# K and V of an attention backward pass, loaded two heads to a transfer

## The chip, the cores and the metric

The kernel runs on one core of a Trainium2 chip. The metric is the device time in microseconds (us) of one execution of the program. The core has five engines that run side by side, each with its own queue of instructions: PE (matrix multiply; PEld is its weight load), DVE (vector work), ACT (scalar engine, used here for copies out of PSUM, one exponential and one scaled copy), POOL (a general engine, used here for a few small products and for issuing stores) and SP (which only issues transfers here). Transfers between the chip's memory (HBM) and the on-chip memory (SBUF, 128 partitions) are carried by 16 DMA engines, which all queues share.

## The reference

Forward and backward of softmax attention in which 32 query heads share 4 key/value heads, for 32 batches:

```python
B, Hq, Hkv, Sq, Sk, D = 32, 32, 4, 4, 2048, 128      # all bf16

def forward(q, k, v):
    k = jnp.repeat(k, Hq // Hkv, axis=1)
    v = jnp.repeat(v, Hq // Hkv, axis=1)
    scores = jnp.einsum("bhqd,bhkd->bhqk", q, k) * D ** -0.5
    p = softmax(scores, axis=-1)
    return jnp.einsum("bhqk,bhkd->bhqd", p, v)

out, vjp = jax.vjp(forward, q, k, v)
return out, *vjp(grad_out)                            # out, dq, dk, dv
```

q, out, grad_out and dq are 1 MB each. k, v, dk and dv are 67.1 MB each: K and V are read once and dK and dV are written once, and these four make up nearly all the traffic.

## The kernel before, in words

One batch is one unit of work. Its 32 query heads of 4 rows give 128 rows, which fill the 128 partitions; 32 rows belong to each of the 4 key/value heads. A head of K (2048 keys of 128 numbers) lies in SBUF as 16 keys to a partition: a partition holds 4 KB of the head, one unbroken piece in HBM, and the head is 512 KB. A batch's K tile has four heads side by side, 16 KB to a partition, 2 MB in all; V's tile has the same shape, and so have the output tiles of dK and dV.

For one batch b the steps are these, named as in the program's table. `LK`, `LV`: issue the loads of K and V. `QDT`: transpose q and grad_out on PE. `KT0` to `KT7` and `VT0` to `VT7`: transpose eight 128x128 blocks of K or V on PE into a bank of PSUM (line 181), then copy them to SBUF on DVE (line 183). An even number takes heads 0 and 1, an odd one heads 2 and 3: `turned` transposes four blocks of the first head of the pair and then four of the second. `Sa`, `Sb`: scores (line 198) and their maxima. `EXa`, `EXb`: the exponential on ACT. `NRM`: row sums, and scaled copies of q and grad_out on POOL. `ETa`, `ETb`: the exponentials transposed. `O`: the output (line 264, reads all of V's tile) and its row-wise product with grad_out. `dPa`, `dPb`: the product of grad_out with V, and dS on DVE (line 350). `dV0` to `dV7`: PE products (line 307), copied out of PSUM by ACT (line 311) into the dV tile. `dSTa`, `dSTb`: dS transposed. `dQ`: line 264 again, reads all of K's tile. `dK0` to `dK7`: as dV.

The order is written out by hand as three lists of step names, `HEAD`, `STEADY` and `TAIL`, and no planner changes it; every engine takes its own share of the steps in that order. `STEADY` is one iteration: steps marked `-` belong to the batch before, `+` to the next, `+2` to the one after that. Its core, as far as the change touches it:

```python
STEADY = """
dSTa- VT4 EXa VT0 QDT+ dSTb- KT4+ dK1- dK6- KT6+ KT2+ KT0+ NRM dK0- dQ- dK3- ... ETb ETa VT7 KT3+ VT6 VT1
dV7 dK4- O dV5 dPb dV1 KT5+ KT1+ dV3 dV6 dPa KT7+ dV2 LK+2 LV+2 VT2+ dV4 Sa+ dV0 Sb+ dK7 VT5+ VT3+ EXb+
"""
```

So the loads of batch b+2 stand at the end of iteration b, and the first transposes of its K (KT4) near the start of iteration b+1. SP has only loads in its queue, so it runs ahead of the other engines and is held by waits alone. There are two kinds. One is for a free buffer: the K tile has three buffers, so K of b+2 waits until `dQ` of b-1 has read its K; the V tile has two, so V of b+2 waits until `O` of b has read its V (and the transposes of V are done). The other is for a semaphore: the framework gives SP's transfers eight semaphores in turn, and a transfer is issued only when the one issued eight before it, which raises the same semaphore, has landed. A batch has eight transfers, so head h of K waits for head h of the batch before, and so with V.

Stores go out on POOL's queue (line 338: dK of a batch in one transfer of 2 MB with four 4 KB pieces to a partition, 512 KB apart in HBM; dV likewise, in some batches cut into parts). dK and dV tiles share four buffers. The first ACT copy into a tile needs the store of the tile four before it to have landed. Each group of four batches has its q and grad_out loaded at once, from SP for the first group and from POOL for the others.

Of the kernel before, what the change touches and what calls it, by code (L numbers as in the profile page):

```python
# [81 lines left out]
def kernel(ctx: ExitStack, tc: tile.TileContext, q, k, v, grad_out, out_0, out_1, out_2, out_3):  # L82
    nc = tc.nc
    B, Hq, Sq, D = q.shape
    NH, Sk = k.shape[1], k.shape[2]
# [41 lines left out]
    k_v = k.rearrange("b h (p c) d -> b h p (c d)", c=C)  # L127
    v_v = v.rearrange("b h (p c) d -> b h p (c d)", c=C)
# [8 lines left out]
    def GROUP(g, queue):  # L137

        groups[g] = []
        for name, src in (("q_sb", q_f), ("do_sb", go_f)):  # L140
            x = qd_pool.tile([P, W, D], BF16, name=name)
            queue.dma_start(out=x[:], in_=src[g * W:g * W + W].rearrange("w p d -> p w d"))
            groups[g].append(x)

    def LK(b):
        S = st[b] = {}
        if b == 0:
            GROUP(0, nc.sync)
        S["q"], S["do"] = (x[:, b % W, :] for x in groups[b // W])
        if b % W == W - 1 and b + 1 < B:  # L150
            GROUP(b // W + 1, nc.gpsimd)
        S["k"] = k_pool.tile([P, NH, C, D], BF16, name="k_sb")
        for h in range(NH):
            nc.sync.dma_start(out=S["k"][:, h].rearrange("p c d -> p (c d)"), in_=k_v[b, h])

    def LV(b):
        S = st[b]
        S["v"] = v_pool.tile([P, NH, C, D], BF16, name="v_sb")
        for h in range(NH):
            nc.sync.dma_start(out=S["v"][:, h].rearrange("p c d -> p (c d)"), in_=v_v[b, h])  # L160

    def bank16():

# [182 lines left out]
    def dP(b, i):  # L346
# [6 lines left out]
        banks.give(t)  # L353

    table = {"LK": LK, "LV": LV, "QDT": QDT, "O": O, "dQ": dQ, "NRM": NRM}
    for i, c in enumerate("ab"):
        for n, f in (("S", S_), ("EX", EX), ("dP", dP), ("ET", ET), ("dST", dST)):
# [8 lines left out]
    for w in STEADY.split():  # L366
        ahead = 0
        for mark, n in (("+3", 3), ("+2", 2), ("+", 1), ("-2", -2), ("-", -1)):
            if w.endswith(mark):
                w, ahead = w[:-len(mark)], n  # L370
# [3 lines left out]
    with tc.manual_schedule():  # L374

        for w in HEAD.split():
            w, b = w.split("@")
# [5 lines left out]
        for w in TAIL.split():  # L383
            w, b = w.split("@")
# [31 lines left out]
```

## Time and profile before

| what | value |
|---|---|
| median of three runs | 690.12 us (684.78 to 690.79) |
| the profiled execution, its own time | 688.33 us |
| span of its trace, first to last instruction | 686.5 us |
| granted TensorE clock, mean | 0.99 |
| PE / DVE / ACT busy | 621.9 / 584.8 / 569.1 us (91 / 85 / 83%) |
| HBM read and written | 136.31 MB and 136.31 MB, 397 GB/s over the span |
| loads of K and V | 128 and 128 transfers of 512 KB from SP's queue |

The profile is one execution. Busy times are sums over the whole span, and the stages of this kernel have different limits: a start that fills the pipeline, a long stretch of like iterations of some 20 us each, and an end in which nothing is loaded any more. The DMA share is the time of all transfer packets over 16 engines' time; packets of one engine overlap a little, so it can come out slightly above 1. A transfer's landing is the moment when the last of the 16 DMA engines has reported its part.

### The profile page before, as it was taken

The page shows a single profiled execution, that of the slowest core. Times are in us where ns is not written, and L with a number is a line of the kernel's source. Part 1 is how long each engine was busy: PE and PEld are TensorE (multiplying, and loading weights), DVE is VectorE, ACT ScalarE, POOL GpSimd, SP SyncE. Part 2 cuts the span into 40 slices and gives each one's busy share as a digit, 9 for nine tenths or more (in the row PEclk, how much of TensorE's full clock was granted, in tenths as well). Part 3 has the DMA queues.
Part 4 walks back from the last instruction along what each step waited for, and adds up shares of the span by engine and source line. Part 5 has one row for each costly group of instructions (what it writes and reads, how often), then busy time and mean ns, then how long its engine had stood idle before and what let it go on. Part 6 is the DMA issues. An engine that isn't in the chain of part 4 may idle for free.

```text
span 686.5 us, 28002 instructions
## 1 busy us (share of the span) xinstructions
PE 621.9 (91%) x12352; PEld 450.2 (66%) x12352; DVE 584.8 (85%) x992; ACT 569.1 (83%) x673; POOL 269.9 (39%) x451
## 2 busy tenths in 40 slices
PE   5899999999999899989899999998999998998981
PEld 4577776667776567766567766666766666665661
DVE  5998999989999889988978889888889888898860
ACT  0698898988889788878788888887888888888894
POOL 1364243544424354432535324454233534324342
PEclk9999999999999999999999999999999999999997
DMA  9999999999999999999999999999999999999967
GB/s 340 405 299 410 416 416 387 415 414 416 415 416 416 414 417 415 417 415 416 416 412 416 415 415 416 410 412 413 417 415 387 406 414 415 417 403 416 368 271 277
DMA packets 75017, 274.44 MB, mean 400 GB/s; under 512 B 8081, under 2 KB 8165, under 8 KB 74896
## 3 DMA queue, kind: packets, MB, share of 16 engines
q0 software_dynamic: 36976, 138.16, 50.3%
q1 hardware_dynamic: 37920, 134.50, 48.8%
q8 instruction: 96, 1.57, 0.8%
q14 instruction: 25, 0.20, 0.1%
HBM read 136.31 MB, written 136.31 MB: 397 GB/s over the span
## 4 chain that ended last, share of the span: by engine, by line
PE 54%; DMA 33%; DVE 4%; issue 3%; ACT 2%; POOL 2%; SPq 0%; POOLq 0%; ACTq 0%; DVEq 0%
DMA k_sb<-in_k_dram 33%; PE banks L181 23%; PE banks L307 14%; PE banks L264 7%; PE banks L198 5%; PE banks L248 5%; ACT dv L311 2%; DVE kt L183 1%; DVE ds L350 1%; POOL dop L231 1%; DVE m L211 1%; DVE vt L183 1%; PE banks L171 1%; POOL out_dram L323 0%; POOL qp L231 0%
## 5 line engine op out<-in xcount | busy, mean ns | idle before, releaser
L311 ACT CAST dv<-banks 128x1024 bf16<-128x1024 f32 x256 | 245.8, 1027 | 44.1 <-PE banks L307 43.6
L311 ACT CAST dk<-banks 128x1024 bf16<-128x1024 f32 x256 | 251.0, 1027 | 33.4 <-PE banks L307 29.1
L183 DVE COPY kt<-banks 128x1024 bf16<-128x1024 bf16 x256 | 165.1, 680 | 11.0 <-PE banks L181 10.9
L231 POOL TENSOR_SCALAR dop<-do_sb,rinv 32x128 bf16<-32x128 bf16 x128 | 76.6, 598 | 234.0 <-DVE rinv L239 119.5
L181 PE MATMUL banks<-ident,k_sb 128*128 128x128 bf16 x2048 | 147.9, 222 | 21.5 <-DMA k_sb<-in_k_dram 15.6
L183 DVE COPY vt<-banks 128x1024 bf16<-128x1024 bf16 x256 | 166.0, 680 | 0.9 <-PE banks L181 0.6
L181 PEld LDWEIGHTS <-k_sb 128*128 128x128 bf16 x2048 | 121.2, 99 | 51.3 <-issue 32.2
L181 PE MATMUL banks<-ident,v_sb 128*128 128x128 bf16 x2048 | 143.0, 219 | 12.7 <-ACT dv L311 10.3
L181 PEld LDWEIGHTS <-v_sb 128*128 128x128 bf16 x2048 | 121.4, 98 | 27.2 <-issue 24.7
L307 PE MATMUL banks<-dop,e 64*128 64x256 bf16 x1024 | 97.4, 273 | 6.6 <-issue 3.9
L350 DVE SCALAR_TENSOR_TENSOR ds<-banks,delta,e 128x1024 bf16<-128x1024 f32 x64 | 82.1, 1283 | 16.9 <-PE banks L198 16.8
L338 POOL DMA_DIRECT2D out_dram<-dv x47 | 33.2, 710 | 147.5 <-ACT dv L311 141.0
L307 PE MATMUL banks<-qp,ds 64*128 64x256 bf16 x1024 | 85.9, 272 | 2.3 <-ACT dk L311 1.4
L231 POOL TENSOR_SCALAR qp<-q_sb,srinv 32x128 bf16<-32x128 bf16 x128 | 77.9, 609 | 10.7
L222 ACT ACTIVATE e<-banks,negb 128x1024 bf16<-128x1024 f32 x64 | 70.7, 1109 | 12.0 <-DVE negb L214 12.0
L211 DVE TENSOR_REDUCE m<-banks 128x1 f32<-128x1024 f32 x64 | 75.1, 1214 | 2.1 <-PE banks L198 1.9
L250 DVE COPY et<-banks 128x1024 bf16<-128x1024 bf16 x64 | 41.3, 686 | 32.7 <-PE banks L248 32.7
L307 PEld LDWEIGHTS <-e 64*128 64x128 bf16 x1024 | 33.2, 94 | 52.4 <-issue 35.6
L307 PEld LDWEIGHTS <-ds 64*128 64x128 bf16 x1024 | 41.5, 94 | 29.4 <-ACT dv L311 12.7
L250 DVE COPY dst<-banks 128x1024 bf16<-128x1024 bf16 x64 | 43.4, 679 | 1.8 <-PE banks L248 1.8
L198 PE MATMUL banks<-vt,qdt 128*32 128x512 bf16 x512 | 40.9, 384 | 1.5 <-issue 1.3
L198 PE MATMUL banks<-kt,qdt 128*32 128x512 bf16 x512 | 39.5, 384 | 0.8 <-DVE vt L183 0.3
(39 smaller groups left out, 458.4 us busy)
## 6 DMA issues: line engine op xcount, KB each, us to landing
k_sb<-in_k_dram SPq DMA_DIRECT2D x128, 512.0 KB, 15.9
v_sb<-in_v_dram SPq DMA_DIRECT2D x128, 512.0 KB, 20.2
out_dram<-dk POOLq DMA_DIRECT2D x31, 2048.0 KB, 22.1
out_dram<-dv POOLq DMA_DIRECT2D x23, 2048.0 KB, 25.8
out_dram<-dv POOLq DMA_DIRECT2D x7, 1440.0 KB, 25.4
out_dram<-dv POOLq DMA_DIRECT2D x7, 512.0 KB, 18.6
out_dram<-dv POOLq DMA_DIRECT2D x3, 1024.0 KB, 6.3
out_dram<-dk POOLq DMA_DIRECT2D x2, 1024.0 KB, 5.6
```

The source lines that it names most:

```text
L181: nc.tensor.transpose(out=ps[:, 4 * hh + j, :], in_=S[which][:, 2 * (i % 2) + hh, 4 * (i // 2) + j, :], identity=ident[:])
L183: nc.vector.tensor_copy(out=S[f"{which}t{i}"][:], in_=ps)
L198: nc.tensor.matmul(ps[G * h:G * h + G, a, :], lhsT=S["qdt"][:, col, G * h:G * h + G], rhs=xt[:, 4 * (h % 2):4 * (h % 2) + 4, :].rearrange( ...
L211: nc.vector.reduce_max(out=S["m"][:, i:i + 1], in_=S[f"s{i}"][1], axis=AX.X)
L222: nc.scalar.activation(out=S[f"e{i}"][:], in_=ps, func=ACT.Exp, bias=S["negb"][:], scale=scale, accum_out=S["l"][:, i:i + 1],)
L231: nc.gpsimd.tensor_scalar(out=t[r, h % 2, :], in0=src[r, :], scalar1=by[r, :], scalar2=None, op0=ALU.mult)
L248: nc.tensor.transpose(out=ps[:, u, :], in_=S[f"{src}{i}"][:, P * u:P * u + P], identity=ident[:])
L250: nc.vector.tensor_copy(out=S[f"{name}{i}"][:], in_=ps)
L264: nc.tensor.matmul(ps[G * h:G * h + G, :], lhsT=S[f"{xt}{c // 8}"][:, c % 8, G * h:G * h + G], rhs=S[kv][:, h, c, :], start=(c == 0), stop ...
L307: nc.tensor.matmul(ps[:, a, :, c, :], lhsT=S[f"{x}{i // 4}"][r, u:u + P], rhs=S[y][r, :, :], start=True, stop=True, tile_position=(2 * G * ...
L311: copy(out=S[name][:, :, 2 * i:2 * i + 2, :].rearrange("p h c d -> p h (c d)"), in_=banks.ap(t).rearrange("p a (j w) -> p (a j) w", j=2),)
L350: nc.vector.scalar_tensor_tensor(out=S[f"ds{i}"][:], in0=ps, scalar=S["delta"][:], in1=S[f"e{i}"][:], op0=ALU.subtract, op1=ALU.mult,)
```

## The change

`LK` and `LV` issue two transfers each instead of four. A transfer takes two neighbouring heads, 1 MB: for each partition the 4 KB piece of the first head and the 4 KB piece of the second, which lie 512 KB apart in HBM and side by side in SBUF. The tiles, their buffers, the steps and their order stay. A batch now has four transfers on SP's queue, so the transfer eight before in that queue is that of the same pair of heads two batches earlier.

```diff
@@ LK
         S["k"] = k_pool.tile([P, NH, C, D], BF16, name="k_sb")
-        for h in range(NH):
-            nc.sync.dma_start(out=S["k"][:, h].rearrange("p c d -> p (c d)"), in_=k_v[b, h])
+        for h in range(0, NH, 2):
+            nc.sync.dma_start(
+                out=S["k"][:, h:h + 2].rearrange("p h c d -> p h (c d)"), in_=k_v[b, h:h + 2].rearrange("h p w -> p h w"),
+            )
@@ LV
         S["v"] = v_pool.tile([P, NH, C, D], BF16, name="v_sb")
-        for h in range(NH):
-            nc.sync.dma_start(out=S["v"][:, h].rearrange("p c d -> p (c d)"), in_=v_v[b, h])
+        for h in range(0, NH, 2):
+            nc.sync.dma_start(
+                out=S["v"][:, h:h + 2].rearrange("p h c d -> p h (c d)"), in_=v_v[b, h:h + 2].rearrange("h p w -> p h w"),
+            )
```

## The prediction

> **What bounds the kernel now.** I first read the table by stages: where the transfers are at their limit, and where not.
>
> ```profile
> core 0: us, PE busy (x) PEld busy (x) DVE busy (x) ACT busy (x) POOL busy (x), PEclk, DMA share, GB/s
> 0.00:20.00 20.00, 11.49 (x142) 9.52 (x143) 11.73 (x19) 3.04 (x4) 2.20 (x12) 1.00 0.92 349
> ...
> 40.00:60.00 20.00, 19.55 (x442) 14.61 (x434) 18.71 (x34) 18.30 (x22) 9.39 (x15) 1.00 0.98 351
> 60.00:80.00 20.00, 18.53 (x359) 13.41 (x351) 17.52 (x32) 17.20 (x22) 7.13 (x12) 1.00 1.03 414
> ...
> 200.00:300.00 100.00, 93.96 (x1846) 67.70 (x1834) 88.75 (x150) 86.30 (x103) 43.02 (x70) 0.98 1.03 415
> ...
> 640.00:660.00 20.00, 19.03 (x384) 13.72 (x381) 16.44 (x28) 18.92 (x24) 9.35 (x17) 1.00 0.86 345
> 660.00:686.50 26.50, 10.77 (x244) 6.68 (x241) 6.68 (x11) 16.99 (x20) 8.73 (x13) 0.81 0.68 255
> ```
>
> The reader is to see the last two columns: from 60 us on, the 16 DMA engines are full (1.03, 414 to 415 GB/s), and they stay so until the loads end near 640. I counted the packets in flight over that stretch: 16.4 on average in nearly every 20 us. No engine has idle time to give. Loads and stores have equal parts in it, by the queues: 50.3% for q0 (stores) and 48.8% for q1 (loads).
>
> Next the chain that ended last, for who feels this.
>
> ```profile
> PE 54%; DMA 33%; DVE 4%; issue 3%; ACT 2%; POOL 2%; SPq 0%; POOLq 0%; ACTq 0%; DVEq 0%
> ```
>
> The 33% is K's loads (226 us). SP's queue has 0%: issuing transfers is nowhere on the chain. In order of time, two turns of the loop read:
>
> ```profile
> 283.49 17.36 DMA k_sb<-in_k_dram
> 300.86 0.05 issue
> 300.90 0.40 PE banks L181 x4
> ...
> 303.61 1.01 PE banks L264 x64
> 304.62 0.34 PE banks L307 x4
> 304.96 0.03 SPq L154
> 304.99 0.04 issue
> 305.04 16.12 DMA k_sb<-in_k_dram
> ```
>
> dQ (L264) frees a K buffer, SP issues K, 16 to 17 us later head 1 of it lands, KT4 finishes its second four transposes (x4: the first four, of head 0, were done before), and so to the next dQ. It looks like a loop of latencies. The landings of single transfers say that it is a queue: K of batch 16 is issued at 304.67, while V of batch 15 still waits in front and lands its four heads at 308.4, 311.1, 313.5 and 315.9; K's follow at 318.5 and 321.2. Loads land 2.5 to 2.6 us apart without a break. Alone in the head of the kernel they land 1.24 to 1.28 us apart (K and V of batch 0 from 7.34 on), so here they get half of the engines, the stores the other half.
>
> How much the transfers cost over the computation: K issues are 19.95 us apart from 100.6 to 200.3 (five batches), when K was hardly waited for, and 20.83 from 200.3 to 616.9 (20 batches). So 20 x 0.88 = 17.6 us is all that better loads could give.
>
> Last, SP's own waits, which the change edits:
>
> ```profile
> SPq L154 <- PE banks L307: 231.1, 29, 12.8
> SPq L160 <- DMA v_sb<-in_v_dram: 137.7, 84, 3.4
> SPq L154 <- DMA k_sb<-in_k_dram: 65.0, 32, 3.7
> SPq L160 <- PE banks L307: 59.7, 28, 4.8
> ```
>
> The lines released by PE are buffer waits, those by a DMA are semaphore waits on the transfer eight before.
>
> **The change, part by part.** The sum is made against the profiled execution: 688.33 us, of which 686.5 is the span; the median is 1.8 us higher.
>
> *Bytes and data packets.* Unchanged: 4 KB pieces, 2048 load packets on each DMA engine, at a median of 159 ns. New is only that an engine alternates between two heads 512 KB apart. The nearest row is the stores, which walk four heads so: their 4 KB packets take 161.8 ns on average between 46 and 640 us, the loads' 161.3. So -0.5 to +0.5 ns a packet, -1 to +1 us; I take 0, since the medians are equal.
>
> *Completion packets.* Each transfer ends with one 4-byte packet on each engine, 9 ns. 128 transfers go, 128 x 9 ns = **-1.2 us** on engines that are full.
>
> *Issues.* 128 of 256 go, and the rest may be longer: one took 0.33 us at least and 0.49 in the median for K, so 0.33 to 0.98 for a double. SP is on no chain, and in the steady state some 10 us of loads lie ahead in the queue: 0. Without that cover, as at the start, two issues took 0.50 + 0.43 us; one double one gives -0.5 to +0.5. I take 0.
>
> *Landing by pairs.* Heads 0 and 1 now land together, when head 1 landed before. Every KT and VT takes both heads of a pair, so the only loss is that its first four transposes can't run ahead. At the start they ran from 5.79 for 0.61 us while head 1 came at 7.34; after the change they stand behind it: bounds 0 and 0.6, I take **+0.4**, since DVE's copies take over the pace at 0.85 us each. In an iteration, four transposes after the landing cost 0.40 us and eight cost 0.61, so +0.2. What hides it: K's next issue is 0.2 us late, but its turn in the queue comes 10 us later. Only the last batch pays, **+0.2**, because from the landing of its head 1 (635.6) to the end there are only engines. Without that cover it is 0.2 for each of the 17 waits of PEld for K, +3.4, or for all 28 steady batches, +6.
>
> *Semaphore waits.* Those of V go (137.7 us in 84 waits, 4.9 us for each batch): the transfer eight before is now two batches old and long landed. What is late next is the buffer: K still waits for dQ (231.1 us), V for O (59.7). V's later heads are issued up to 7 us sooner, into a queue that is never empty and keeps its order. A place further back in a full queue is worth nothing: 0. The bounds are far apart, -17.6 (the excess above) and +19 (stores displaced, below); I take 0 by the row nearest to it, the DMA share of 1.03.
>
> Sum: 688.3 - 1.2 + 0.4 + 0.2 = 687.7, **688 us**.
>
> Two rules of the Trainium skill bear on this. "DMA: Bandwidth & Descriptors", section "Bandwidth", says to batch to 1 MiB or more, and its section on the anatomy of one DMA gives each a fixed 2.0 us. By that the sum would lose up to 128 x 2.0 = 256 us, if nothing overlapped. The trace disagrees: 512 KB transfers queued behind one another landed 1.27 us apart at the start, 412 GB/s, so the fixed part is covered already.
>
> **The rivals.**
>
> *Faster: the leading engines may run on.* The 16 reports of one load are spread over 6 to 13 us after 200 us: some DMA engines are far ahead of the slowest. They take a load early only if it is issued, and V's semaphore waits tied issue to the slowest engine's landing. With the waits gone they could do loads sooner and leave stores to the end, where the share falls to 0.86 and 0.68. Against it: a batch is released by the slowest engine, whose queue always held loads. Half of the 17.6 us would give 688 - 9 = 679.
>
> *Slower: stores come late.* Place: the first ACT copy into an output tile (L311), which needs the store four tiles before. From the trace that store landed 2.6 us before at the least, 4.8 in the lowest quarter, 5.8 in the median. If loads issued 4.9 us sooner push stores back by as much, it decides from 2.6 us on: a quarter of 60 tiles, 15, would stall by 4.9 - 3.6 = 1.3 us, +19 us at most; half of that as PE's slack takes some: 698. For it: the margins are small, and no ACT wait on a store shows now. Against: the share of two full queues isn't changed by what stands further back.
>
> *Slower: the jumps of 512 KB cost.* Each ns on a load packet is 2048 ns on every engine, +2 us; from 3.4 ns on it is over 1%. At 5 ns, 3% of a packet, it is +10: 698. Against it speaks the stores' row, 0.5 ns. The same page of the Trainium skill, "Latency and other measured facts", has copies between HBM tensors at 207 GB/s with rows 512 KiB apart and 214 with a padded pitch, some 3% apart; no run here shows such a copy, and its jumps lie between partitions, not within one.
>
> *The landing by pairs is not hidden:* +6, 694; it needs a loop of latencies in place of a queue.
>
> *It isn't what it says:* were the double transfer split or spread over fewer DMA engines, the list of issues would show it; K alone on half of the engines would double its 2.6 us a head, far outside. The stores have the same shape, and all 16 engines reported the first of them within 0.3 us.
>
> **How the numbers follow.** Forecast 0.55, pairs not hidden 0.11, leading engines 0.14, late stores 0.11, jumps 0.07, not what it says 0.02. One per cent, 6.9 us, is about what a measurement of this kernel can tell from none: the runs shown differ by 6.0. So faster 0.14, same 0.66, slower 0.20. The forecast's own range is 683 to 693, the spread of runs on top of the small terms. For 8 in 10 I reach to the faster rival at 679 and, on the slower side, to 698 and a little over: 678 to 700.
>
> **What would show it.** Right: a DMA share of 1.02 to 1.03 from 60 to 640 us with 128 loads of 1024 KB; no semaphore waits under SP's V line, with its waits for PE grown instead; K's issue to landing longer but still a third of the chain; x8 in place of x4 after it. Wrong: a share under 1.02 in the steady part, ACT waiting for a store, load packets off 159 ns, or K leaving the chain. My sum fails if the spread between DMA engines, which I count at nothing, turns out to set the pace.

## The result, and the profile after

| | before | after |
|---|---|---|
| median of 20 runs each | 690.02 us (684.78 to 693.28) | 690.83 us (689.05 to 698.88) |
| ratio after / before, 95% interval | | 1.0043 (1.0025 to 1.0062) |
| the profiled execution, its own time / its span | 688.33 / 686.5 us | 691.81 / 690.0 us |
| PE idle between 60 and 640 us, released by K's loads | 13.3 us | 0 |
| ACT idle in its copies, released by a store | 0 | 21.7 us |
| POOL idle, released by a store | 0 | 12.3 us |
| last load of K or V landed, and from there to the end | 650.8, 35.7 us | 649.2, 40.8 us |

By the ratio, the change costs 0.43%, some 3 us. The two medians alone are 0.8 us apart and the two means 2.3: runs of one kernel scatter by several us, and 8 of the 20 runs of before lie under 689 us but none of after. So the loss is small and its size is rough, yet the interval excludes zero. Behind it stands a large exchange: the wait for K, which carried a third of the chain before, is gone, and waits for stores have come in its place.

First the table by stages of the changed kernel, with the columns as before.

```profile
core 0: us, PE busy (x) PEld busy (x) DVE busy (x) ACT busy (x) POOL busy (x), PEclk, DMA share, GB/s
60.00:80.00 20.00, 19.30 (x394) 13.92 (x386) 18.10 (x32) 17.70 (x22) 7.13 (x12) 1.00 1.03 414
...
200.00:300.00 100.00, 91.18 (x1815) 65.53 (x1804) 86.97 (x147) 85.05 (x102) 43.01 (x70) 0.99 1.03 416
...
600.00:640.00 40.00, 35.70 (x686) 25.84 (x683) 33.53 (x56) 32.93 (x40) 15.07 (x25) 1.00 1.01 387
640.00:660.00 20.00, 19.19 (x410) 13.72 (x407) 18.48 (x32) 18.42 (x23) 7.25 (x12) 1.00 0.84 337
660.00:690.00 30.00, 13.91 (x319) 9.23 (x312) 7.80 (x14) 20.45 (x24) 11.33 (x18) 0.85 0.67 251
```

The reader is to see that up to 400 us nothing has happened to the DMA engines as a whole: 1.03 and 414 to 416 GB/s, as before. Later they move a little less: 387 GB/s from 600 to 640 us, where before has 410:

```profile
600.00:640.00 40.00, 35.75 (x731) 25.24 (x728) 34.79 (x60) 32.83 (x41) 12.87 (x21) 1.00 1.02 410
```

A second profile of the changed kernel has its dip elsewhere (404 from 400 to 500 us, 416 from 600 to 640). Over 60 to 640 us both profiles of the changed kernel have 412 GB/s, the two of before 413 and 414.

The chain that ended last, by engine, and then one turn of it in order of time (start, us, what):

```profile
PE 55%; DMA 26%; ACT 5%; POOL 5%; issue 4%; DVE 4%; POOLq 0%; SPq 0%; ACTq 0%; DVEq 0%
```

```profile
267.76 0.65 POOL out_dram L298
268.41 29.37 DMA out_dram<-dk
297.78 0.02 issue
297.80 0.04 ACTq L315
297.84 0.04 issue
297.88 1.02 ACT dk L315
```

Before, the DMA share of the chain was K's loads. Now nearly all of it is stores of dK. In the turn shown, POOL issues one at 268.41, it lands 29.37 us later, and ACT's first copy into that buffer (line 315 is line 311 of before) starts at once. The view of waits says how often (waiting instruction <- what released it: us in all, times, longest us):

```profile
POOL out_dram L342 <- DMA out_dram<-dk: 12.3, 3, 6.3
PE banks L252 <- ACT dk L315: 11.4, 10, 1.8
ACT dv L315 <- DMA out_dram<-dv: 11.1, 6, 3.2
ACT dk L315 <- DMA out_dram<-dk: 10.6, 9, 1.8
...
PEld L185 <- DMA k_sb<-in_k_dram: 2.9, 1, 2.9
```

ACT waits 15 times for a store, and PE then waits for ACT (second line: the transposes of dS, queued behind the copies). The one wait for K left is that of the start. PE's own waits for K, before first and after second, were:

```profile
PE banks L181 <- DMA k_sb<-in_k_dram: 15.6, 15, 2.2
PE banks L185 <- DMA k_sb<-in_k_dram: 2.7, 1, 2.7
```

SP's own waits, and the list of transfers (last number: median us from issue to landing), show that the change does what it says:

```profile
SPq L154 <- PE banks L311: 419.4, 29, 18.3
SPq L162 <- PE banks L311: 131.8, 30, 12.5
...
SPq L162 <- DMA v_sb<-in_v_dram: 0.6, 1, 0.6
```

```profile
k_sb<-in_k_dram SPq DMA_DIRECT2D x64, 1024.0 KB, 13.7
v_sb<-in_v_dram SPq DMA_DIRECT2D x64, 1024.0 KB, 17.4
out_dram<-dk POOLq DMA_DIRECT2D x31, 2048.0 KB, 25.9
```

V's semaphore waits went from 137.7 us to 0.6, and the waits for a buffer grew. K lands after 13.7 us; the kernel before had 15.9 for a half of that size. A store of dK takes 25.9 us; before it took 22.1.

### The profile page after: what moved, and what is told of

Same layout as the page of the kernel before. It is cut to its first block, busy times and chain, and to the rows that moved or that the text cites. A ratio compares the mean times of both kernels' runs of the same rounds, so it can differ in the third digit from the quotient of the medians.

```text
span 690.0 us, 27874 instructions
## 1 busy us (share of the span) xinstructions
PE 621.9 (90%) x12352; PEld 453.8 (66%) x12352; DVE 585.3 (85%) x992; ACT 568.9 (82%) x673; POOL 270.0 (39%) x451
## 3 DMA queue, kind: packets, MB, share of 16 engines
q0 software_dynamic: 36976, 138.16, 50.1%
q1 hardware_dynamic: 35872, 134.49, 48.5%
## 4 chain that ended last, share of the span: by engine, by line
PE 55%; DMA 26%; ACT 5%; POOL 5%; issue 4%; DVE 4%; POOLq 0%; SPq 0%; ACTq 0%; DVEq 0%
DMA out_dram<-dk 25%; PE banks L185 24%; PE banks L311 13%; PE banks L252 7%; PE banks L268 7%; PE banks L202 4%; ACT dv L315 4%; POOL qp L235 2%; DVE kt L187 1%; POOL dop L235 1%; ACT dk L315 1%; DVE ds L354 1%; DMA k_sb<-in_k_dram 1%; PE banks L175 1%; POOL out_dram L298 1%
## 5 line engine op out<-in xcount | busy, mean ns | idle before, releaser
L185 PE MATMUL banks<-ident,v_sb 128*128 128x128 bf16 x2048 | 143.8, 220 | 13.3 <-ACT dv L315 10.2
L185 PE MATMUL banks<-ident,k_sb 128*128 128x128 bf16 x2048 | 144.4, 221 | 7.2 <-issue 3.2
L185 PEld LDWEIGHTS <-v_sb 128*128 128x128 bf16 x2048 | 122.9, 98 | 27.7 <-issue 26.8
L354 DVE SCALAR_TENSOR_TENSOR ds<-banks,delta,e 128x1024 bf16<-128x1024 f32 x64 | 82.1, 1283 | 21.7 <-PE banks L202 19.8
L252 PE MATMUL banks<-ident,ds 128*128 128x128 bf16 x512 | 39.9, 223 | 11.7 <-ACT dk L315 11.4
## 6 DMA issues: line engine op xcount, KB each, us to landing
k_sb<-in_k_dram SPq DMA_DIRECT2D x64, 1024.0 KB, 13.7
v_sb<-in_v_dram SPq DMA_DIRECT2D x64, 1024.0 KB, 17.4
out_dram<-dk POOLq DMA_DIRECT2D x31, 2048.0 KB, 25.9
```

Of the source, the lines that this page charges most:

```text
L185: nc.tensor.transpose(out=ps[:, 4 * hh + j, :], in_=S[which][:, 2 * (i % 2) + hh, 4 * (i // 2) + j, :], identity=ident[:])
L252: nc.tensor.transpose(out=ps[:, u, :], in_=S[f"{src}{i}"][:, P * u:P * u + P], identity=ident[:])
L354: nc.vector.scalar_tensor_tensor(out=S[f"ds{i}"][:], in0=ps, scalar=S["delta"][:], in1=S[f"e{i}"][:], op0=ALU.subtract, op1=ALU.mult,)
```

## The experiments

Two questions stood at the start. Why do loads gain on stores when both queues are full? And why does that cost time? There are two theories for the first. By **the hold**, the semaphore waits of SP throttled the loads, and with them gone V enters the queue earlier and takes the stores' place. By **the turn**, each DMA engine alternates between the load queue and the store queue packet by packet, and the 4-byte packet that ends a transfer takes a whole turn, in which the other queue moves 4 KB. A 512 KB load is 8 data packets and 1 ending on each engine, so 9 turns; a 1 MB load has 17 for 16; a 2 MB store 33 for 32. Fewer endings would then give the loads a larger part of the same bandwidth, whatever SP waits for.

In the expectations the hold is theory A. Theory B is a cost of the double transfers themselves, C an accident of one execution, D a small cost outside the waits on stores. The turn is theory E; it was put up only when twelve of these runs were done, so that it stands in the expectations from the bare queues on, and what the earlier runs say for it is read into them afterwards.

Ratios are to runs of the kernel before on the same chip. "K waits" is PE's idle time released by K's loads between 60 and 640 us; "store waits" is ACT's idle time released by a store, then POOL's. "dK's store" and "dK landing" are the median time from issue to landing over all stores of dK. "Landing gap" is the time between the landings of consecutive 512 KB of loads in the full stretch, median.

### The kernel before once more

The kernel of before, unchanged, to see how far a ratio and the waits wander.

> The kernel before once more, for a second trace. Theory A (the semaphore waits of V's loads hold the loads back and so give the stores their share; without them the stores come late and the four output buffers stop ACT): ratio 1.000 within 0.003, PE waits for K of 15 to 40 us in all, no ACT or POOL wait on a store. Theory B (the double transfer itself, its landing by pairs and its jumps, costs the 0.4%): the same here. Theory C (the late DMA engine in the first trace was an accident of that execution, and the two kernels differ by nothing that repeats): waits of another kind than in the first trace, K waits under 10 us or ACT waiting for stores.

Measured: 688.17 us, 1.0005 (0.9982 to 1.0028). K waits 13.1 us, store waits 0 and 0, dK's store 23.1 us in the median by its landings. So the K waits repeat, and a ratio of 1.004 isn't drift.

### Pairs with an ending added, heads with an ending added

To each 1 MB transfer a tiny one is added, 16 rows of 4 bytes, one to each DMA engine: 2 turns (its data packet and its ending), next to no bytes.

```diff
 # pairs_tiny, against after
+    def TINY(b):
+        x = tiny_pool.tile([16, 2], BF16, name="tiny")
+        nc.sync.dma_start(out=x[:], in_=q_f[b, 0:16, 0:2])
...
 # in LK and in LV, after each dma_start of two heads
+            TINY(b)
```

> Transfers of 1 MB, and behind each a tiny one (16 partitions of 4 bytes), so that a batch again takes eight semaphores and a pair of heads waits for the same pair of the batch before. The 128 tiny ones cost every DMA engine two packets of some 9 ns, +2.3 us at most. Theory A: the K waits of PE are back (15 to 40 us), ACT's and POOL's waits on stores under 3 us in all, stores of dK land after some 22 us in place of 25.9; the time 690 to 692, ratio to before 1.000 to 1.003, and under that of the changed kernel in spite of the added packets. Theory B: the waits don't matter, the cost of the pairs stays: 1.004 + 0.003 = 1.007. Theory C: anything from 0.998 to 1.006, with waits that don't follow the edit.

Measured: 694.22 us, 1.0078 (1.0056 to 1.01). Store waits 0 and 0, K waits back at 15.8 us, landing gap 2.645 us against 2.55 for plain pairs, dK's store landing after 15.4 us instead of 25.9. From its view of waits and its list of transfers:

```profile
PEld L193 <- DMA k_sb<-in_k_dram: 22.0, 16, 3.6
```

The waits of the kernel before are back, in a kernel whose loads are still 1 MB, from bytes that don't count. This run can't tell the two theories apart: the tiny transfers take semaphores as well, so a batch has eight again, and the hold asks for the same waits. Its time, 1.0078, lies above theory A's range (up to 1.003) and near theory B's 1.007. Of it, the added packets' own time is 2.3 us at most (an estimate: 256 packets of 9 ns on each engine); also, to make room, the scratch tile of `O` has one buffer in this kernel and the next, in place of three. The same tiny transfer behind each head of V in the kernel before:

```diff
 # heads_tiny, against before: in LV, after each dma_start of one head
+            TINY(b)
```

> The kernel before with a tiny transfer behind each head of V, so that a batch takes twelve semaphores and each load is tied to one nearer before it: a stronger hold on the loads than before, with transfers of 512 KB. The same +2.3 us at most for the tiny packets. Theory A: loads later still, K waits of PE over 40 us in all, no wait on a store, stores of dK landing sooner than 22.1 us; the time at or over before plus the packets, 1.003 to 1.012. Theory B: 1.003, only the packets, with K waits as before.

Measured: 696.22 us, 1.0101 (1.0078 to 1.0125). K waits 17.4 us, store waits 0 and 0, dK's store 15.2 us. The landing gap is 2.80 us for V, 2.95 in the upper quartile, and for K, which has no tiny transfer, 2.63 as before. Its view of waits (which counts the whole span and PE's weight loads by themselves, so that its sums are larger than the K waits above) has 34 waits for K where before has 17:

```profile
PEld L188 <- DMA k_sb<-in_k_dram: 29.1, 34, 2.4
```

So endings and semaphores together move the limit from the stores to the loads, and the pace moves only for the transfers that carry the endings.

### K alone by pairs

```diff
 # k_pairs, against after: V as before
-        for h in range(0, NH, 2):
-            nc.sync.dma_start(
...
+        for h in range(NH):
+            nc.sync.dma_start(out=S["v"][:, h].rearrange("p c d -> p (c d)"), in_=v_v[b, h])
```

> Only K by pairs, V by heads of 512 KB: six transfers to a batch, so heads 0 and 1 of V wait for a K transfer of the batch before (long landed) and heads 2 and 3 for heads 0 and 1 of V of the batch before, which land two transfers sooner than what they waited for till now. Most of the hold is gone while V's transfers stay as they were. Theory A: near the changed kernel, 1.002 to 1.006, ACT waits on stores of 5 us or more, few K waits. Theory B: half of the cost, 1.001 to 1.003, K waits as before.

Measured: 689.77 us, 1.0024 (1.0008 to 1.004). Landing gap 2.547 us for K and 2.627 for V. K waits 0, store waits 19.0 and 1.5 us:

```profile
ACT dk L313 <- DMA out_dram<-dk: 11.7, 8, 3.0
ACT dv L313 <- DMA out_dram<-dv: 7.3, 5, 1.9
```

Half of the change already turns the waits round, for about half of the loss. Both theories allow it: 9.6 us of SP's semaphore waits are left of 202.7.

### More room for the output tiles

If the store waits are the loss, a fifth output buffer or more slack in the four should remove it. To make room in SBUF for it, the transposed tiles of V share one tile and four of K's share two. **What this leaves out:** the score products and the product of grad_out with V then read blocks that aren't their own; the count of instructions and transfers stays. Two kernels keep four output buffers with that room unused (the controls), two have five.

```diff
 # heads_out4s / pairs_out4s (4 buffers), heads_out5 / pairs_out5 (outp bufs=5)
-    kt_pool = ctx.enter_context(tc.tile_pool(name="ktp", bufs=8))
-    vt_pool = ctx.enter_context(tc.tile_pool(name="vtp", bufs=8))
+    kt_pool = ctx.enter_context(tc.tile_pool(name="ktp", bufs=6))
+    vt_pool = ctx.enter_context(tc.tile_pool(name="vtp", bufs=1))
...
+        same = 0 if which == "v" else {1: 4, 7: 6}.get(i, i)
```

> Control for the next three. To make room, K's transposed blocks use six buffers instead of eight and V's one instead of eight; the score products then read blocks that are not their own (KT1 overwrites KT4, KT7 overwrites KT6, all VT share one), so scores and what follows hold other numbers; every instruction, its size and its order stay, and no new wait comes up, since all writers are DVE and all products stand after the blocks. Transfers by heads, four output buffers. Both theories: ratio 1.000 within 0.003 of before, the same waits: PE for K 10 to 20 us, none on stores.

> As the control, with the room used for a fifth output buffer; transfers by heads. Theory A (loads held back by semaphores, stores with room to spare, so the fifth buffer is not needed): within 0.002 of the control. Theory D (the small cost of the pairs lies at the start and the end, not in waits on stores): the same.

> The changed kernel with the same room-making as in the control (score products read blocks that are not their own), four output buffers. Both: like the changed kernel, 1.002 to 1.006 against before, ACT and POOL waiting 15 to 35 us for stores.

> The changed kernel with the same room-making and a fifth output buffer. Theory A: the waits on stores vanish or fall under 5 us, and with them the cost: 0.995 to 1.001 against before, so 0.4% or more under the four-buffer pairs; faster than both kernels if the loads' lead then holds to the end. Theory D: no better than four buffers within 0.002, 1.002 to 1.006.

| | us | ratio | K waits | store waits | dK landing |
|---|---|---|---|---|---|
| heads, four buffers, shared tiles | 690.36 | 1.0055 (1.0027 to 1.0083) | 3.8 | 0 / 0 | 21.4 |
| heads, five buffers | 690.04 | 1.0045 (1.0016 to 1.0073) | 3.6 | 0 / 0 | 20.0 |
| pairs, four buffers, shared tiles | 692.39 | 1.0064 (1.003 to 1.0098) | 0 | 1.9 / 0 | 21.8 |
| pairs, five buffers | 691.87 | 1.0075 (1.0043 to 1.0108) | 0 | 0 / 0 | 23.9 |

These four are **inconclusive**. Sharing the tiles isn't neutral: the heads' control is 0.55% slower than the kernel before, with some 8 us of new waits of PE for DVE, since a transpose must now wait until the tile it shares has been read. Computation that is slower itself needs less bandwidth, so both kinds of waits shrink, and the fifth buffer has little left to remove. Within them, pairs lie 0.1 to 0.3% above heads, but the intervals overlap. Theory A had the fifth buffer bring the pairs to 0.995 to 1.001: the store waits did vanish, and the time (1.0075) did not fall. So a cost of the pairs outside the waits on stores (theory D) isn't excluded by these.

### The same hold on V, in both kernels

This separates the hold from the turn. In both kernels V's tile gets a small write by DVE before its loads, so that V is issued when DVE comes to that place, and not when a semaphore lets it. In the first column of the next view stands the start of an issue, then its length; x2 and x4 are the transfers.

```diff
 # pairs_vlate against after, heads_vlate against before: in LV
         S["v"] = v_pool.tile([P, NH, C, D], BF16, name="v_sb")
+        if b > 1:
+            nc.vector.memset(S["v"][:, 0, 0, 0:2], 0.0)
```

> The changed kernel once more, for a second trace and a second ratio. Theory A (V's semaphore waits gone, loads run ahead, stores late, ACT and behind it PE wait for output buffers): 1.002 to 1.006, ACT waits on stores of 10 to 25 us, no K waits. Theory D (a cost of the pairs that has nothing to do with waits on stores): the same ratio. Theory C (accident of one execution): waits of another kind.

> The changed kernel, with one small DVE memset of two elements a partition into V's tile, put where LV stands in DVE's order, so that V's load of b+2 is issued when DVE gets to the end of iteration b and not at once when O has read the old V: a hold on V that asks nothing of the transfers. Cost of 30 memsets of some 0.1 us on DVE: 3 us on an engine that is 85% busy, mostly hidden. Theory A: ACT's and POOL's waits on stores under 5 us, some K waits back, 0.999 to 1.002. Theory D: 1.003 to 1.006 as without the hold.

> The kernel before with the same memset, as the control of its cost. V's loads by heads were held by semaphores already; now the first ones are issued later too. Both theories: 1.000 to 1.004, K waits of 10 to 30 us, no waits on stores. It is to be set beside the pairs with the same hold: Theory A has the two equal within 0.002, Theory D the pairs 0.003 above.

SP's queue, of pairs first and of heads second:

```profile
282.99 1.81 SPq L154 DMA_DIRECT2D k_sb<-in_k_dram  x2
293.82 1.42 SPq L164 DMA_DIRECT2D v_sb<-in_v_dram  x2
```

```profile
284.86 2.74 SPq L154 DMA_DIRECT2D k_sb<-in_k_dram  x4
295.32 2.02 SPq L162 DMA_DIRECT2D v_sb<-in_v_dram  x4
```

V goes out 10.8 us behind K in the one and 10.5 in the other, K at once in both: the hold is the same. The waits, pairs first and heads second:

```profile
ACT dk L317 <- DMA out_dram<-dk: 8.9, 5, 3.0
POOL out_dram L344 <- DMA out_dram<-dk: 6.4, 2, 6.1
ACT dv L317 <- DMA out_dram<-dv: 4.5, 3, 1.8
```

```profile
PEld L183 <- DMA k_sb<-in_k_dram: 21.0, 19, 2.4
PE banks L183 <- DMA k_sb<-in_k_dram: 17.6, 19, 2.3
```

| | us | ratio | K waits | store waits | landing gap, K / V | dK landing |
|---|---|---|---|---|---|---|
| after, once more | 691.92 | 1.0041 (1.0012 to 1.007) | 0 | 12.5 / 7.5 | 2.553 / 2.515 | 23.6 |
| pairs, V held | 694.24 | 1.0078 (1.0047 to 1.0109) | 0 | 13.4 / 6.4 | 2.546 / 2.552 | 25.4 |
| heads, V held | 689.52 | 1.0015 (0.9985 to 1.0045) | 15.2 | 0 / 0 | 2.625 / 2.626 | 21.2 |

With V issued alike, pairs wait for stores and heads wait for K. SP has no semaphore wait left in the pairs and 28.0 us of them in the heads, where before has 202.7 us; yet the heads' K waits are 15.2 us, no less than the 13.3 of before. Theory A had the store waits of the pairs under 5 us and the time at 0.999 to 1.002; both missed. **The hold falls** as what turns the waits round. The ratio of after repeats (1.0043, then 1.0041). The held pairs are 0.6% above the held heads, more than the 0.4% between the kernels without the hold; why was not found.

### V alone by pairs

The mirror of K alone.

```diff
 # v_pairs, against before
-        for h in range(NH):
-            nc.sync.dma_start(out=S["v"][:, h].rearrange("p c d -> p (c d)"), in_=v_v[b, h])
+        for h in range(0, NH, 2):
+            nc.sync.dma_start(
...
```

> Only V by pairs, K by heads: six transfers to a batch; V waits for K's heads 2 and 3 of the batch before, long landed, so V has no hold at all, and K's transfers are as before. Theory A: like the changed kernel, 1.002 to 1.006, ACT waits on stores of 10 us or more, K waits under 5. Theory D: half of the cost, 1.000 to 1.003, whatever the waits.

Measured: 689.34 us, 1.0025 (0.999 to 1.0059). Landing gap 2.623 us for K and 2.543 for V: now V has the faster pace. K waits 0.3 us, store waits 14.8 and 12.2. K comes early enough although its own transfers are those of before, so what relieves it lies in the one queue that both share. V has no hold at all here, so theory A asks for the same; with the hold fallen, the pace is what is left.

### The two queues bare

No computation: POOL issues 72 stores of 2 MB of zeros, SP issues the loads in four stretches of eight batches each, by heads, by pairs, by fours, and by heads with a tiny transfer behind each. Outputs are zeros, and nothing is computed; eight of the stores are extra, so its time is not compared.

```diff
+        for n in range(72):
+            b = n // 2 % B
+            nc.gpsimd.dma_start(out=(dk_v if n % 2 else dv_v)[b], in_=outs[n % 4][:].rearrange("p h c d -> p h (c d)"))
+        for b in range(B):
+            step, tiny = ((1, False), (2, False), (4, False), (1, True))[b // 8]
+            LOAD(k_pool, "k_sb", k_v, b, step, tiny)
+            LOAD(v_pool, "v_sb", v_v, b, step, tiny)
```

> No computation: 72 stores of 2 MB of zeros into dK and dV from POOL's queue, never empty, beside all loads of K and V from SP's queue, in four phases of 8 batches: transfers of one head, of two, of four, and of one head each followed by a tiny transfer. Nothing of out and dq but zeros is written. A 4 KB packet takes 155 ns of a full engine. Theory E (packets take turns, a completion packet has a turn; a store has 33 turns for 32 data packets): 512 KB of loads land every 8 x 0.155 + 9 turns of the stores at 0.1506 = 2.60 us by heads, 2.52 by pairs, 2.49 by fours, 2.93 by heads with tiny ones (11 turns). If turns don't count and bytes are shared evenly: 2.49 to 2.52 in all four. If it is a fixed cost of a transfer on the load queue of some other kind: the fourth phase near the first.

First the two queues (q0 stores, q1 loads: packets, MB, share of 16 engines) while heads (60 to 150 us), pairs (170 to 310) and heads with tiny ones (490 to 640) were moved.

```profile
q0 software_dynamic: 4977, 19.78, 53.4%
q1 hardware_dynamic: 4975, 18.09, 49.1%
```

```profile
q0 software_dynamic: 7535, 29.95, 52.0%
q1 hardware_dynamic: 7534, 29.03, 50.5%
```

```profile
q0 software_dynamic: 9057, 35.97, 58.3%
q1 hardware_dynamic: 9055, 26.90, 44.4%
```

This is the turn itself: whatever the size of a load, both queues move the same number of packets, endings counted, to within 3; by fours (330 to 470 us) it is 7425 and 7428. It holds beside computation too: from 200 to 400 us the kernel before has 11130 packets of q0 and 11186 of q1, its second profile 11153 and 11154. The changed kernel has 11151 and 10548 there: its loads had at times less to send than their turns.

Next two stretches of SP's queue. Each issue there is held until the transfer eight before it has landed, in all four stretches alike, so issues follow the pace of landings.

```profile
93.11 8.12 SPq L119 DMA_DIRECT2D k_sb<-in_k_dram  x4
103.55 8.12 SPq L119 DMA_DIRECT2D v_sb<-in_v_dram  x4
```

```profile
529.50 0.33 SPq L119 DMA_DIRECT2D v_sb<-in_v_dram  x1
529.87 0.46 SPq L124 DMA_DIRECT2D tiny<-in_q_dram  x1
532.46 0.33 SPq L119 DMA_DIRECT2D v_sb<-in_v_dram  x1
...
535.28 0.33 SPq L119 DMA_DIRECT2D k_sb<-in_k_dram  x1
```

Four heads go out in 10.44 us, 2.61 each; with the tiny transfer they come 2.96 and 2.82 us apart. The total stays at 419 to 421 GB/s, so what the loads lose the stores gain. The part of the bytes that the turn gives is counted so: in one turn a load moves 8/9, 16/17, 32/33 or 8/11 of a packet, a store always 32/33.

| loads by | data packets / turns | loads' part, counted | measured, GB/s of loads and of stores | loads' part, measured | us per 512 KB, mean |
|---|---|---|---|---|---|
| heads | 8 / 9 | 47.8% | 201, 220 | 47.8% | 2.61 |
| pairs | 16 / 17 | 49.2% | 207, 214 | 49.2% | 2.525 |
| fours | 32 / 33 | 50.0% | 211, 211 | 50.0% | 2.49 |
| heads and a tiny one | 8 / 11 | 42.9% | 179, 240 | 42.8% | 2.92 |

The fours' 2.49 is a median. The count meets the measurement to 0.1 points in all four, with nothing fitted. The packet's own time, 9 ns, has no share in this: what it costs is the other queue's 4 KB packet, some 0.15 us. "DMA: Bandwidth & Descriptors" of the Trainium skill, section "Queues, rings and completion order", has each DMA engine alternate between the queues that have work, packet by packet; the trace agrees. It gives a packet as 9 to 17 descriptors as a rule; by the counts here a turn goes with each 4 KB piece, and with each ending.

### Further the same way: V in one transfer

```diff
 # v_whole, against after
-        for h in range(0, NH, 2):
+        for h in range(0, NH, NH):
```

> The changed kernel with V loaded as one transfer of 2 MB, K by pairs. Theory E: V lands at 2.49 us for 512 KB in place of 2.54, the loads' part grows once more, dK's stores land 0.5 us or more later than the 25.9 and 23.6 us of the changed kernel, ACT waits on stores of 15 to 40 us, no K waits; time 1.003 to 1.010 against before. If the part of the loads has nothing to do with the number of transfers: as the changed kernel.

Measured: 693.54 us, 1.0086 (1.0047 to 1.0125). Landing gap 2.42 us for V (mean 2.46), 2.55 for K. K waits 0, store waits 18.5 and 7.3 us, dK's store 25.8 us. V's pace rises again. The loss is twice that of after by the ratios, though the intervals overlap, and the stores land no later than in after, which theory E had not expected. So part of this loss isn't seen in the landings of stores; where it comes from is open.

### The change from batch 20 on, and half of it

```diff
 # pairs_late, against after: in LK and in LV
+        step = 2 if b >= 20 else 1
-        for h in range(0, NH, 2):
+        for h in range(0, NH, step):
```

> Heads up to batch 19, pairs from batch 20 on. Theory E: up to some 400 us as before, with K waits; then the loads get the larger part and use up the 3 to 6 us by which stores land early in the kernel before; K waits of PE fall under 10 us, ACT waits on stores come only near the end and stay under 8 us. Both margins used: 0.996 to 1.001 against before, under the changed kernel in any case. If the pairs cost something by themselves: 1.001 to 1.003.

Measured: 690.22 us, 1.0018 (0.9997 to 1.004). K waits 4.5 us, store waits 11.2 and 7.2. In its view of waits both kinds stand together:

```profile
PEld L187 <- DMA k_sb<-in_k_dram: 10.8, 10, 3.0
...
ACT dk L317 <- DMA out_dram<-dk: 7.2, 5, 1.9
```

They lie one after the other: the last wait for K is at 383.6 us, the first wait for a store at 505. By the pace of before (K of batch 16 issued at 304.67, 20.83 us a batch), batch 20 is issued near 388. So K's waits stop where the size changes, and stores take some 120 us, about six batches, to fall behind. The store waits came to more than the 8 us expected, and the time to more than the 0.996 to 1.001: using both margins gained nothing.

The last kernel looks for a better point in between: V by pairs in every second batch only, K by heads.

```diff
 # v_pairs_odd, against before: in LV
+        step = 2 if b % 2 else 1
-        for h in range(NH):
+        for h in range(0, NH, step):
...
```

> V by pairs in odd batches only, K and V by heads otherwise. The load queue takes 36 turns for 32 data packets in even batches and 34 in odd ones, 35 on average, between 36 of the kernel before and 34 of V by pairs. If the split is all: at the end K is ready 0 to 4 us before its use and the stores land 0.5 to 3 us before their buffer's next use, waits for K of 2 to 10 us and for stores under 8 us, 0.998 to 1.001 against before. If pairs cost something besides: 1.001 to 1.003.

Measured: 688.58 us, 1.0003 (0.9984 to 1.0022). K waits 4.8 us, store waits 11.5 and 6.2, more than the 8 us expected. It is as fast as the kernel before and no faster; no kernel here beat that one.

### All splits side by side

| turns per 512 KB of loads, mean of K and V | kernel | ratio | K waits | store waits (ACT / POOL) | dK landing |
|---|---|---|---|---|---|
| 8.375 | K pairs, V whole | 1.0086 (1.0047 to 1.0125) | 0 | 18.5 / 7.3 | 25.8 |
| 8.5 | after | 1.0043 (1.0025 to 1.0062) | 0 | 21.7 / 12.3 | 25.9 |
| 8.75 | K alone by pairs | 1.0024 (1.0008 to 1.004) | 0 | 19.0 / 1.5 | 25.8 |
| 8.75 | V alone by pairs | 1.0025 (0.999 to 1.0059) | 0.3 | 14.8 / 12.2 | 25.0 |
| 8.875 | V by pairs every second batch | 1.0003 (0.9984 to 1.0022) | 4.8 | 11.5 / 6.2 | 24.4 |
| 9 | before, once more | 1.0005 (0.9982 to 1.0028) | 13.1 | 0 / 0 | 23.1 |
| 9.5 | pairs and tiny ones | 1.0078 (1.0056 to 1.01) | 15.8 | 0 / 0 | 15.4 |
| 10 | heads, tiny ones with V | 1.0101 (1.0078 to 1.0125) | 17.4 | 0 / 0 | 15.2 |

The reader is to see one line with a lowest point. Fewer turns, and stores are late; more turns, and loads are late. The kernel before lies at the bottom, within what these runs can tell. The waits follow the turns; the time doesn't follow them alone. The pairs with V held have 8.5 turns as after has, and 1.0078, and the two kernels with tiny transfers carry added packets.

## Why the prediction was right or wrong

The time forecast, 688.0, is 2.8 us under the measured 690.83; the range holds it, and a change within 1% was the likeliest class. The sign is wrong: a gain of 0.6 us was forecast against the profiled execution, and 0.43% was lost. The forecast's case, "nothing much happens", didn't come about: two large effects nearly cancelled, so that the time came out near the forecast by luck.

**What bounds the kernel.** Right, and the runs confirm it: the DMA engines are full in both kernels for most of the loop, and the loop of latencies was a queue. It explains why an exchange of tens of microseconds of waits moves the end by 3. The compute phase of 19.95 us a batch wants 8.52 MB in that time, 427 GB/s; the kernels get 414 to 416. The shortfall must show as a wait somewhere, and the split between the queues says on which side.

**"Loads and stores have equal parts in it, by the queues: 50.3% ... and 48.8%".** This reading hid the split. The row is a total over the whole span, and follows the bytes of each queue (138.16 and 134.50 MB), which the program fixes: the changed kernel has 50.1% and 48.5%. How two full queues share the engines can't be read from it. It shows in the pace while both are full: 2.62 us for 512 KB against the 1.27 of the start is 48.5% for the loads, not a half.

**Completion packets, -1.2 us.** This is the step that failed. It took 128 packets by their own 9 ns and left the parts of the two queues as they were. Each ending also passes a turn to the stores, and without them the loads' pace went from 2.62 to 2.55 us per 512 KB in the median. Over the 256 pieces of K and V that would be 18 us of lead, at the stores' expense, if the load queue stayed full. It doesn't: buffers stop the loads, the last one lands at 649.2 us against 650.8, and over 60 to 640 us the loads' part of the bytes is 49.2% against 49.1%. What moves is when loads and stores land, and with it who waits. The total bandwidth doesn't rise, so nothing is gained, and where -1.2 us was forecast the kernel lost some 3.

**Semaphore waits, 0.** As far as it goes, right: with V held alike, heads still wait for K and pairs for stores. "What is late next is the buffer" is right too: SP's waits for PE went from 231.1 to 419.4 us for K and from 59.7 to 131.8 for V. The lower bound, -17.6, asked what better loads could give. Earlier loads did come, and K's 13.3 us of waits went, but the gain was taken back by the stores, which that bound didn't charge.

**The rival "stores come late".** It had the right place, the first ACT copy into an output tile, and the right sign. Its cause was wrong (loads issued sooner), and the argument against it, that the share of two full queues isn't changed, was the error. Its size was too large: 15 stalls of 1.3 us were priced at +19 at most and taken at +10; 15 waits came, 21.7 us on ACT, and 3 us remained at the end. What was left out is that the same mechanism removes the waits for K. PE's idle time between 60 and 640 us, by what released it:

| | K | ACT | issue | sum |
|---|---|---|---|---|
| before | 13.3 | 8.9 | 13.3 | 35.5 |
| before, once more | 13.1 | 8.9 | 10.5 | 32.5 |
| after | 0 | 25.0 | 13.6 | 38.6 |
| after, once more | 0 | 18.1 | 19.1 | 37.2 |

The sum rises by 3.1 us between the first profiles of the two kernels, but it can't carry the loss: the two profiles of before differ by 3.0 us in it, with spans 0.1 us apart. Why the new waits cost 3 us more than those they replace is only argued, and theory D isn't excluded. Loads that land ahead of their need are bytes that stores could have used. In the batches 27 to 31, K's head 1 lands 3.7 to 9.3 us before KT4 needs it in after, and 0.0 in before; after its last load the changed kernel still needs 40.8 us against 35.7 (43.3 against 37.3 in the second profiles). Yet V by pairs in every second batch also needs 40.7 us there and ends as early as before. In before, stores land at least 2.6 us ahead of need (1.0 in the second profile), a smaller waste of the same kind.

**The leading engines.** The spread of one load's 16 reports (last less median; medians of 100 us stretches from 300 to 600 us) did fall, from 4.9 to 6.4 us down to 1.8 to 3.0. But that of dK's stores rose from 4.9 to 6.8 up to 9.3 to 10.4. The second profiles say the same (3.9 to 6.1 down to 1.5 to 4.3, and 4.3 to 7.1 up to 8.4 to 9.5). The lag of the last reports moved to the stores, and no time was gained. (From first to last report, a load in before takes 6 to 17 us after 200 us, more than the 6 to 13 of the prediction.)

**The jumps of 512 KB.** The 5 ns didn't come: load packets take 159 ns in the median in both kernels, and in the mean from 46 to 640 us 161.3 before and 161.6 after (161.0 and 162.0 in the second profiles), beside 161.8 and 162.0 for stores. The bare queues move 421 GB/s by heads and by pairs.

**Landing by pairs.** The +0.4 at the start can't be told: batch 3's K is issued at 41.47 instead of 40.95 us, but in the second profiles at 41.34 instead of 42.34, so that two profiles of before differ by more than the term. By batch 5 the first profiles are level (80.98 and 80.94). That the pairs aren't hidden, +6, didn't occur: the waits for K that would have paid it were gone.

**Issues.** Nothing speaks against 0: an issue of 1 MB takes 0.47 to 0.50 us in the median, and SP stays at 0% of the chain.

**The signs named.** "ACT waiting for a store" and "K leaving the chain" were both named as what would prove the forecast wrong, and both are in the profile. The DMA share of 1.02 and the packet of 159 ns, named as right, held as well; neither could see the split.

The rule that the prediction weighed also asks for a word. By the Trainium skill, "DMA: Bandwidth & Descriptors", section "Bandwidth", transfers of 1 MiB or more are to be preferred. Here the larger transfer did raise the pace of its own queue, by 2.7% (2.62 to 2.55 us), at the cost of the other, and the kernel lost 0.4%. The fixed 2.0 us that the prediction set beside it stands in the Trainium skill for transfers issued from gpsimd, while these go out from SP.

## What to carry to other kernels

When two DMA queues are full at once, count packets rather than bytes: here both queues moved equally many, the ending of every transfer was a turn given away, and so a larger transfer sped its own queue and slowed the other. Before making transfers larger, look which side has slack: a margin of 1.0 to 2.6 us on the stores was spent by a shift that is 1.4 points between two full queues. And where the engines are full, a wait that goes is no gain until it is known which wait takes its place.

## What the runs showed of the hardware

- Two full queues moved equally many packets, to within 3 of some 5000 to 9000, for every size of load.
- The 4-byte packet that ends a transfer takes 9 ns, yet passes a turn worth some 0.15 us to the other queue. A transfer of 16 times 4 bytes, 2 turns, slowed the loads by 0.31 us for each 512 KB (2.61 to 2.92), while the total stayed at 419 against 421 GB/s.
- The two queues alone move 421 GB/s, beside computation 414 to 416.
- The 16 DMA engines don't report one transfer together, and which queue shows the lag changes with the split: the spread of dK's reports is 9.3 to 10.4 us in after and 1.4 to 1.8 in the pairs with tiny transfers, where the loads' is 6.0 to 7.9.
